# Placing gate passes after each half of a column tile, in a gated recurrence followed by a multiplicative feed-forward

## The chip, the core and the metric

The kernel runs on one core of a Trainium2 chip. The metric is device time in microseconds (us) of one execution. Engines are named as in the profile: PE (TensorE matmul, with PEld for its weight loads), DVE (VectorE), ACT (ScalarE), POOL (GpSimd), SP (SyncE, which here issues nearly all DMAs).

## The reference, cut to what matters

Batch 4, 8 heads, 768 positions, head dimension 48. A recurrence with a complex gate per position and row, then a feed-forward of two products multiplied together:

```python
mag = np.sqrt(a_re * a_re + a_im * a_im)
scale = np.minimum(mag, 0.999) / (mag + 1e-06)
a_re_n, a_im_n = (a_re * scale, a_im * scale)
for t in range(S):
    ar, ai = (a_re_n[:, :, t, :, None], a_im_n[:, :, t, :, None])
    new_re = ar * S_re - ai * S_im
    new_im = ar * S_im + ai * S_re
    kv = np.einsum('bhd,bhe->bhde', k[:, :, t], v[:, :, t])
    S_re, S_im = (new_re + kv, new_im)
    y[:, :, t] = np.einsum('bhd,bhde->bhe', q[:, :, t], S_re)
# x = y as (3072 tokens, 384)
a = x @ w1            # 384 x 1024
b = x @ w2
out = (a * b @ w3) @ w_out
```

The weights come as 64-bit floats; the rest is float32.

## The kernel before

The recurrence is solved in closed form over a **unit** of 384 positions (half a sequence of one batch; 8 units, `NU`; "tile u" or "unit u" below). The running product of gate magnitudes is a scan, the running sum of gate angles is another, and with k divided and q multiplied by the running product and both turned by the angle, the recurrence becomes a masked product of q and k. The feed-forward's w3 and w_out are multiplied into one matrix `w3o` beforehand, in the prologue.

**What PE does for a unit** (`pieces`, L1108): per chunk of 128 positions (3, `UC`) two transposes `tp` of the turned keys (`turn`, L724), copied by ACT into `KT` (L733); the state product `kv` (`state`, L787; its sum `T` is made by DVE at L802, or by an ACT copy at L800); scores `sc` (`scores`, L736; DVE puts them under the mask at L748); outputs `y` (`outputs`, L760; ACT copies them into `xT`, L781). `tp`, `kv` and `y` share two PSUM buffers, so each needs the reader of the one before the last to be done. Odd units have no state product for the last chunk.

**The feed-forward of the unit before** is laid between these pieces: `ffn_ab` (L813), 8 column tiles, each two groups of three 128x384 matmuls (L820; w1 first, then w2), an ACT copy `a` (L825) and a DVE product `ab` (L826), in four PSUM buffers; then the output product. For unit 0 that is three chunks of 8 matmuls (`ffn_out`, L901, L909); for later units the last chunk so, and the first two by seven smaller products `p` (`out_pair`, L851, L873), for which DVE first makes four sums `So` (L848) and adds the results (L855).

**Gates** of the next unit (`gates`, L563) run on ACT and DVE meanwhile, whole passes over 128x1152 elements (unit 0: three parts of 384). Each is yielded with its engine, an estimated cost, a name and the names that it waits for. Their order before: Ln and Exp of re (names a1, r1; `act`, L576), im/re (L591), range looks on re (`low`, ACT, `check_gates`, L548, into Z), square and maximum (L598), Ln (z1), n (L608), z2, a2, z3 on ACT, min (L619), three scans (mag, L624), Ln and Exp of the running product (l, e: the `gR` rows of L576), q (L636), z4 (L638), r2 (L640), k (L642), three tiny copies (ends, L645), table load and arctangent (at, L648), three angle scans (ang, L655), turns (ACT) and z5 (L667), abs, cos, sin (ACT), then kc, qc, ks, qs (L682 to L691). The load of the next `re` follows the angle scans, of the next `im` kc and qc. Then 12 DMAs move the results into `KL` and `QL` (`move`, L701), and k and q of the next unit are loaded.

**What sets the order.** PE's order is written out by hand. In the prologue the other engines are ordered by the framework's scheduler from the order of emission. From the end of unit 0's pieces on, all engines follow the order in which `run` (L1171) emits: it walks the list of PE items; after each it emits gate passes as long as a planner with clocks per engine (costs in `TIMES`, L1142, and in the yields) finds that the pass starts before the next item's PE work ends and is done before its engine is next asked for (`fits`, L1226). So gate passes stand only between items, and `ab`, with both its groups, is one item. `AHEAD` says how many items of the feed-forward come before the unit's first piece; `HEAD` how many `ab` items come before unit 1. Each engine runs its queue in that order.

**Prologue** (to 85.5 us): eight rows of w3 and w_out are converted from 64-bit words (ACT L955, L958; DVE L951, L953, L961, L963, L965) and multiplied by PE (`fuse`, L1070) while unit 0's gates run; then unit 0's pieces with the first gate passes of unit 1 (`step`), and four blocks of w1 and w2 (`w12_work`; `raw` loads at L936), of which the last two are converted within unit 0's feed-forward (kind `abw`).

**Checks.** POOL reads the weights and gates again (`check_weights`) for values outside a range; `judge` (L1078) gathers all tests on DVE, sums them by one small matmul (`count`, L1097) and leaves a verdict in `good`; every engine reads it at the end (L1356), and a general path runs if it is 0.

Of the kernel before, what the change touches and what calls it, by code (L numbers as in the profile page):

```python
# [375 lines left out]
def kernel(  # L376
# [47 lines left out]
    HEAD = 8  # L424
# [6 lines left out]
    AHEAD = [0, 0] + [4] * (NU - 2)  # L431
    LO, HI = 32, D - 32
    PASS, WIDE, SCAN, LAND, SLACK, LATE, RING, LOOK = 1.17, 1.36, 0.97, 1.8, 0.7, 1.2, 8, 4.0
# [114 lines left out]
    def check_gates(u, re, junk, f=0):  # L548
        return [nc.scalar.activation(out=junk, in_=re, func=AF.Relu, scale=scale, bias=bias,
                                     accum_out=st_low[:, x, u, f:f + 1])  # L550
                for x, (scale, bias) in enumerate(((-1.0, LEAST), (1.0, MOST)))]
# [11 lines left out]
    def gates(u, split):  # L563
# [25 lines left out]
        for i, s in enumerate(parts):  # L589
            yield "DVE", WIDE, "im", ("r1", ("im", u))  # L590
            tt(out=im[:, s], in0=im[:, s], in1=r[:, s], op=OP.mult)  # L591
            if u > 1:
                yield "ACT", 2.5, "low", ("r1",)
                check_gates(u, re, Z)
        yield None
        for i, s in enumerate(parts):
            yield "DVE", WIDE, "sq", ("im", "low")
            nc.vector.tensor_tensor_reduce(out=Z[:, s], in0=im[:, s], in1=im[:, s], scale=1.0, scalar=0.0,  # L598
                                           op0=OP.mult, op1=OP.max, accum_out=st_tan[:, u, i:i + 1])
# [17 lines left out]
        for s in parts:  # L617
            yield "DVE", 0.76, "min", ("a2",)
            least = ts(out=A[:, s], in0=A[:, s], scalar1=0.999, scalar2=None, op0=OP.min)  # L619
            if u == 1:  # L620
                tc.add_manual_dep(least.ins, masked[-1].ins.name, ORDER, reason="scores first")
            for f in range(s.start, s.stop):
                yield "DVE", SCAN, "mag", ("min", "z3")
                nc.vector.tensor_tensor_scan(out=A[:, f], data0=A[:, f], data1=Z[:, f], initial=1.0,  # L624
                                             op0=OP.mult, op1=OP.mult)
        yield None
# [7 lines left out]
        for s in parts:  # L634
            yield "DVE", WIDE, "q", ("mag", ("q", u))
            tt(out=q[:, s], in0=q[:, s], in1=A[:, s], op=OP.mult)  # L636
            yield "DVE", WIDE, "z4", ("e",)
            tt(out=Z[:, s], in0=A[:, s], in1=r[:, s], op=OP.mult)  # L638
            yield "DVE", WIDE, "r2", ("z4",)
            stt(out=r[:, s], in0=Z[:, s], scalar=2.0, in1=r[:, s], op0=OP.subtract, op1=OP.mult, reverse0=True)  # L640
            yield "DVE", WIDE, "k", ("r2", ("q", u))
            tt(out=k[:, s], in0=k[:, s], in1=r[:, s], op=OP.mult)  # L642
        yield "ACT", 0.6, "ends", ("k",)
        for X in (R[:, :, TT], K2[:, :, TT], st_dec[:, u]):
            nc.scalar.copy(out=X, in_=A[:, :, TT - 1])  # L645
        yield None
        yield "ACT", 2.45, "at", ("im",)
        chain(nc.scalar.preload_act_table_set("trig_and_small"))  # L648
        for s in parts:
            act(out=im[:, s], in_=im[:, s], func=AF.Arctan)  # L650
        yield None
# [10 lines left out]
        for s in parts:  # L662
            n = re[:, s].bitcast(I32)
            yield "ACT", PASS, "turns", ("ang",)
            act(out=n, in_=Z[:, s], func=AF.Copy, scale=0.5 / PI)
            yield "DVE", WIDE, "z5", ("turns",)
            stt(out=Z[:, s], in0=n, scalar=-2 * PI, in1=Z[:, s], op0=OP.mult, op1=OP.add)  # L667
# [116 lines left out]
    for T in Tb:  # L784
        nc.gpsimd.memset(T, 0.0)
# [27 lines left out]
    def ffn_ab(u, j):  # L813
        if j == 0:
            ab_t[u] = one.tile([P, KF, TT], FP, tag="ab", name="ab")
        got = []
        for w in (w1s, w2s):
            m = ps_m.tile([P, TT], FP, tag="mm", name="m")
            for f in range(KD):
                nc.tensor.matmul(out=m, lhsT=w[:, j * P // WB, f, j * P % WB:j * P % WB + P], rhs=xT_t[u][:, f],  # L820
                                 start=(f == 0), stop=(f == KD - 1))
            got.append(m)
        a = two.tile([P, TT], FP, tag="a", name="a")
        with tc.high_priority():
            nc.scalar.copy(out=a, in_=got[0])  # L825
            nc.vector.tensor_tensor(out=ab_t[u][:, j], in0=got[1], in1=a, op=OP.mult)  # L826
# [278 lines left out]
    for V in Vb:  # L1105
        nc.gpsimd.memset(V, 0.0)

    def pieces(u):  # L1108
# [6 lines left out]
        if u % 2:  # L1115
            return [[("need", u), tr[0][0]], [tr[0][1]], [tr[1][0], kv[0]], [tr[1][1]], [kv[1]], sc[0], sc[1] + [y[0]],
                    sc[2] + [y[1]], [y[2], ("end", u)]]
        return [[("need", u), tr[0][0]], [tr[0][1]], [tr[1][0], kv[0]], [tr[1][1]], [tr[2][0], kv[1]], [tr[2][1]],
                [kv[2]] + sc[0], sc[1] + [y[0]], sc[2] + [y[1]], [y[2], ("end", u)]]

    def ffn(u, parts=1):
        ab = [("ab", lambda j=j: ffn_ab(u, j)) for j in range(KF)]
        last = [("o" if n == parts - 1 else "part", f) for n, f in enumerate(ffn_out(u, UC - 1, parts))]
        if u == 0:
            return ab + [(("part", "o")[n], f) for t in range(UC) for n, f in enumerate(ffn_out(u, t, parts))]
# [5 lines left out]
    def unit(u, rest, ahead):  # L1131
# [5 lines left out]
        first = [i * (len(rest) - 2) // (n - 1) for i in range(n)] + [len(rest)] if u > 1 else [0, 1, 2, 3, 3, 4, 4, 5, 5, 5, 6]  # L1137
# [5 lines left out]
        "ab": (("PE", 1.94), ("ACT", 0.48), ("PE", 1.94), ("DVE", 0.56)),  # L1143
        "abw": (("PE", 1.94), ("ACT", 0.48), ("PE", 1.94), ("DVE", 0.56), ("DVE", 0.56), ("ACT", 1.08), ("DVE", 1.5)),
# [3 lines left out]
        "part": (("PE", 2.58),), "p1": (("PE", 1.3), ("ACT", 0.32)), "p2": (("PE", 1.3),), "p4": (("PE", 1.3),),  # L1148
# [22 lines left out]
    def run(seq):  # L1171

        def item(kind):
# [11 lines left out]
            if k in ("ab", "abw", "so", "spart", "part", "p1", "p2", "p7", "p5"):  # L1185
                wait = held["m"][-4]
                held["m"].append(clock["PE"] + (8.0 if k[0] == "p" else 0.0))
            clock["PE"] = max(clock["PE"], wait)
            for e, d in TIMES[kind]:
                if e != "PE":  # L1190
                    done = max(done, clock["PE"])
                elif k in ("ab", "abw") and done:
                    clock["PE"] = max(clock["PE"], held["m"][-4])
                    held["m"].append(0.0)
# [6 lines left out]
                if e != "PE" and k in ("ab", "abw", "so", "o"):  # L1201
                    held["m"][-1] = done
# [75 lines left out]
    with tc.manual_schedule(engines={mybir.EngineType.PE}):  # L1278
# [36 lines left out]
        for i, p in enumerate(pieces(0)):  # L1315
# [3 lines left out]
            if i in (1, 3, 6, 9):  # L1319
# [6 lines left out]
            step(steps, 5 if i == 0 else i >= 6)  # L1326
            if i in (5, 7):
                work[2 + (i == 7)]()
        with tc.manual_schedule(engines={mybir.EngineType.Activation, mybir.EngineType.DVE, mybir.EngineType.Pool, mybir.EngineType.SP}):
# [4 lines left out]
            def head(i):  # L1334
                rest[i][1]()
                if i in (2, 3):
                    work[2 + i]()
                if i == 4:
# [5 lines left out]
            seq = [("abw" if i in (2, 3) else "ab", lambda i=i: head(i)) for i in range(HEAD)]  # L1344
# [4 lines left out]
            clock.update(POOL=0.0, SP=0.0, DMA=0.0)  # L1349
            ready.clear()  # L1350
            ready.update(at=6.5, r2=6.3, k=7.7)
            advance()
            run(seq[:-6] + [("judge", 0)] + seq[-6:-2] + [("judge", 1)] + seq[-2:])
# [41 lines left out]
```

## Time and profile before

| what | us |
|---|---|
| median of 3 runs (561.05 to 562.63) | 562.1 |
| the profiled execution, its own time | 560.6 |
| its span on the core | 558.7 |
| PE busy | 524.4 |
| last PE matmul ends | 549.96 |

In a row of the profile stand the line of the kernel, the engine, the operation, out<-in with sizes, then busy time and what ended the idle time before it. "issue" is time in which the engine waited for nothing that the profile shows. The slices row gives the busy share in tenths of 40 equal parts of the span. Where PE is idle for a short time its releaser is named, with how long and how often.

### The profile page before, as it was taken

Reading aid. Unit: us, or ns where it says so; the run is one execution under the profiler, and the core shown is the slowest. Engines: PE = TensorE matmul, PEld = TensorE weight load, DVE = VectorE, ACT = ScalarE, POOL = GpSimd, SP = SyncE. Lnnn points to the kernel's source line nnn. Section 1 sums busy time; section 2 is a strip of 40 time slices with the busy share of each in tenths; the row PEclk is TensorE's granted clock in tenths of the full one; section 3 lists DMA queues with packets and bytes.
Section 4 is the critical chain, followed back from the end, with each engine's and each line's share of the span. In section 5 each row is a group of like instructions: output and inputs, shape, how many; then the busy total and the mean of one; then the engine's idle time right before and its main releaser. Section 6 shows DMA issues by size and latency. Waiting matters only on the chain.

```text
span 558.7 us, 13227 instructions
## 1 busy us (share of the span) xinstructions
PE 524.4 (94%) x5474; PEld 358.8 (64%) x5474; DVE 364.0 (65%) x514; ACT 274.8 (49%) x389; POOL 362.7 (65%) x425
## 2 busy tenths in 40 slices
PE   4779889998999999999999999999999999999993
PEld 2345565566656785669666875687567856696572
DVE  7998399778685866687576756695848664421141
ACT  6988766585377325742475237722774242111100
POOL 3000000198888888888899889898998888886000
PEclk9899979999999999999999999999999999999998
DMA  8996978279559626892579245943595228322001
GB/s 260 354 406 166 285 210 279 65 167 196 137 125 242 182 106 174 204 265 77 145 192 222 83 118 152 241 130 102 136 234 156 64 69 212 77 70 70 0 2 49
DMA packets 73190, 89.73 MB, mean 161 GB/s; under 512 B 31776, under 2 KB 62944, under 8 KB 72352
## 3 DMA queue, kind: packets, MB, share of 16 engines
q1 hardware_dynamic: 67040, 69.78, 47.2%
q0 software_dynamic: 6080, 19.01, 11.6%
q8 instruction: 45, 0.74, 0.6%
q14 instruction: 25, 0.20, 0.1%
HBM read 65.14 MB, written 4.72 MB: 125 GB/s over the span
## 4 chain that ended last, share of the span: by engine, by line
PE 79%; DVE 8%; ACT 5%; issue 2%; DMA 2%; SPq 1%; DVEq 0%; ACTq 0%
PE m L820 45%; PE p L873 11%; PE y L779 7%; PE o L909 6%; PE sc L745 5%; DVE So L848 2%; PE kv L796 2%; DVE gA L624 2%; PE tp L731 2%; PE f L1070 1%; ACT gZ L576 1%; ACT low L955 1%; DMA im<-in_a_im_dram 1%; DMA k<-in_k_dram 1%; ACT gR L576 1%
## 5 line engine op out<-in xcount | busy, mean ns | idle before, releaser
L820 PE MATMUL m<-xT,w1s 128*128 128x384 f32 x384 | 135.0, 488 | 0.0
L820 PE MATMUL m<-xT,w2s 128*128 128x384 f32 x384 | 134.3, 486 | 0.0
L820 PEld LDWEIGHTS m<-xT,w2s 128*128 128x128 f32 x384 | 73.0, 190 | 50.9
L820 PEld LDWEIGHTS m<-xT,w1s 128*128 128x128 f32 x384 | 71.4, 190 | 44.9
L826 DVE TENSOR_TENSOR ab<-m,a 128x384 f32<-128x384 f32 x64 | 35.4, 553 | 91.4 <-PE m L820 83.1
L1016 POOL TENSOR_SCALAR look<-look 128x256 f32<-128x256 f32 (+1 forms) x84 | 88.4, 1053 | 7.3
L997 POOL TENSOR_TENSOR seen<-seen,look 128x256 bf16<-128x256 bf16 (+1 forms) x84 | 69.5, 828 | 6.8
L825 ACT COPY a<-m 128x384 f32<-128x384 f32 x64 | 30.3, 473 | 77.8 <-PE m L820 77.8
L981 POOL MEMSET seen<- 128x256 bf16 x1 | 0.3, 312 | 101.9 <-DVE w2s L965 101.9
L1013 POOL TENSOR_TENSOR look<-look 128x256 f32<-128x256 f32 (+1 forms) x72 | 59.5, 826 | 1.9
L909 PE MATMUL o<-w3o,ab 128*128 128x384 f32 x160 | 54.1, 487 | 0.0
L1015 POOL TENSOR_SCALAR look<-look 128x256 f32<-128x256 f32 (+1 forms) x44 | 50.4, 1146 | 5.1 <-DMA look<-in_a_re_dram 1.9
L781 ACT COPY xT<-y 128x384 f32<-128x384 f32 x24 | 11.4, 477 | 76.6 <-PE y L779 76.6
L992 POOL DMA_DIRECT2D look<-in_w_dram x56 | 33.6, 599 | 16.6 <-POOL seen L997 16.6
L733 ACT COPY KT<-tp 128x384 f32<-128x384 f32 x40 | 34.0, 856 | 18.1 <-PE tp L731 17.9
L1018 POOL TENSOR_TENSOR look<-look 128x256 f32<-128x256 f32 (+1 forms) x44 | 39.4, 896 | 3.7
L748 DVE COPY_PREDICATED A<-mask,sc 128x512 f32<-128x512 uint8 x48 | 33.0, 732 | 13.3 <-PE sc L745 12.8
L909 PEld LDWEIGHTS o<-w3o,ab 128*128 128x128 f32 x160 | 29.5, 190 | 18.3 <-issue 0.2
L779 PE MATMUL y<-A,V 128*32 128x128 f32 x768 | 40.2, 278 | 0.0
L1070 PE MATMUL f<-wo_s,w3s 128*128 128x384 f32 x96 | 37.2, 534 | 1.6 <-issue 1.6
L745 PE MATMUL sc<-QL,KL 96*32 96x32 f32 (+3 forms) x1536 | 33.5, 239 | 4.1 <-DVE A L748 1.9
L745 PEld LDWEIGHTS sc<-QL,KL 96*32 96x32 f32 x1536 | 29.2, 112 | 10.6 <-DVE A L748 4.4
(121 smaller groups left out, 904.7 us busy)
## 6 DMA issues: line engine op xcount, KB each, us to landing
look<-in_w_dram POOLq DMA_DIRECT2D x56, 256.0 KB, 3.5
raw<-in_w_dram SPq DMA_DIRECT2D x6, 1024.0 KB, 10.2
raw<-in_w_dram SPq DMA_DIRECT2D x8, 768.0 KB, 8.9
KL<-gR SPq DMA_DIRECT2D x24, 192.5 KB, 5.0
KL<-k SPq DMA_DIRECT2D x24, 192.5 KB, 5.6
re<-in_a_re_dram SPq DMA_DIRECT2D x24, 192.0 KB, 3.4
im<-in_a_im_dram SPq DMA_DIRECT2D x24, 192.0 KB, 3.3
k<-in_k_dram SPq DMA_DIRECT2D x24, 192.0 KB, 8.8
```

Source lines behind the costliest of these rows:

```text
L745: nc.tensor.matmul(out=sc[SB * g:SB * g + SB, j, s0:C], lhsT=KL[:, x * n + j, w][:, s0:s0 + SB], rhs=QL[:, x * n + j, w][:, s0:C], start=T ...
L779: nc.tensor.matmul(out=o, lhsT=a, rhs=b, start=s0, stop=s1)
L820: nc.tensor.matmul(out=m, lhsT=w[:, j * P // WB, f, j * P % WB:j * P % WB + P], rhs=xT_t[u][:, f], start=(f == 0), stop=(f == KD - 1))
L826: nc.vector.tensor_tensor(out=ab_t[u][:, j], in0=got[1], in1=a, op=OP.mult)
L873: nc.tensor.matmul(out=m[p], lhsT=a[:, f], rhs=b[:, f], start=(f == 0), stop=(f == KH - 1))
L909: nc.tensor.matmul(out=m, lhsT=ab_t[u][:, f, t * P:(t + 1) * P], rhs=w3o[:, f], start=(f == 0), stop=(f == KF - 1))
L997: nc.gpsimd.tensor_tensor(out=seen[:, 0:n], in0=seen[:, 0:n], in1=x, op=OP.add)
L1013: tt(out=x, in0=x, in1=x, op=OP.mult)
L1015: ts(out=y, in0=x, scalar1=high, scalar2=None, op0=OP.is_le)
L1016: ts(out=x, in0=x, scalar1=low, scalar2=None, op0=OP.is_ge)
L1018: tt(out=x, in0=x, in1=y, op=OP.mult)
L1070: nc.tensor.matmul(out=sums[j], lhsT=w3_t[f][:, j * P:(j + 1) * P], rhs=w3_t["wo"][:, f], start=(f == 0), stop=(f == KF - 1))
```

## The change

Each group of three matmuls of `ffn_ab` becomes an item of its own ("ab1" with the ACT copy, "ab2" with the product), so that the planner may put gate passes and pieces after either. `HEAD` and `AHEAD` now count halves; some costs and start clocks of the planner are changed. In the gates: the two range looks go from behind r1 to the scans, one after each of the first two, and write their junk into the `gR` buffer; for units from 1 on, the table load and arctangent stand right behind l and e, followed by z4 and r2; k, q and the three tiny copies come after the angle scans and the turns pass. In unit 0, q comes after k. In `pieces` the last two outputs of a unit stand together. Output chunks in two parts get the kind "half". The verdict's tests are emitted before the `ab2` group of column tile 6, and its count before that of column tile 7, in the last unit's feed-forward. Two memsets on POOL clear only the columns that no load writes.

```diff
-    HEAD = 8
+    HEAD = 16
-    AHEAD = [0, 0] + [4] * (NU - 2)
+    AHEAD = [0, 0, 12, 10] + [8] * (NU - 4)
-    PASS, WIDE, SCAN, LAND, SLACK, LATE, RING, LOOK = 1.17, 1.36, 0.97, 1.8, 0.7, 1.2, 8, 4.0
+    PASS, WIDE, SCAN, LAND, SLACK, LATE, RING, LOOK = 1.17, 1.4, 1.05, 1.8, 0.7, 1.2, 8, 4.0
...
-            if u > 1:
-                yield "ACT", 2.5, "low", ("r1",)
-                check_gates(u, re, Z)
...
-            yield "DVE", WIDE, "sq", ("im", "low")
+            yield "DVE", WIDE, "sq", ("im",)
...
+                if u > 1 and f < 2:
+                    yield "ACT", 1.25, "low", ("im",)
+                    check_gates(u, re, r, f)
...
-        for s in parts:
-            yield "DVE", WIDE, "q", ("mag", ("q", u))
-            tt(out=q[:, s], in0=q[:, s], in1=A[:, s], op=OP.mult)
+        def spread(s):
             yield "DVE", WIDE, "z4", ("e",)
             tt(out=Z[:, s], in0=A[:, s], in1=r[:, s], op=OP.mult)
             yield "DVE", WIDE, "r2", ("z4",)
             stt(out=r[:, s], in0=Z[:, s], scalar=2.0, in1=r[:, s], op0=OP.subtract, op1=OP.mult, reverse0=True)
+
+        def scaled(s):
             yield "DVE", WIDE, "k", ("r2", ("q", u))
             tt(out=k[:, s], in0=k[:, s], in1=r[:, s], op=OP.mult)
+            yield "DVE", WIDE, "q", ("mag", ("q", u))
+            tt(out=q[:, s], in0=q[:, s], in1=A[:, s], op=OP.mult)
...
+        early = u > 0
+        if early:
+            yield "ACT", 2.45, "at", ("im",)
+            chain(nc.scalar.preload_act_table_set("trig_and_small"))
+            bent(parts[0])
+            yield from spread(parts[0])
+            yield None
+        else:
+            for s in parts:
+                yield from spread(s)
+                yield from scaled(s)
+            yield from ends()
...
             yield "ACT", PASS, "turns", ("ang",)
             act(out=n, in_=Z[:, s], func=AF.Copy, scale=0.5 / PI)
+            if early:
+                yield from scaled(s)
+                yield from ends()
...
-        nc.gpsimd.memset(T, 0.0)
+        nc.gpsimd.memset(T[:, :, D:64], 0.0)
...
+        return [("ab1", lambda: half(w1s)), ("ab2", lambda: half(w2s))]
...
-                    sc[2] + [y[1]], [y[2], ("end", u)]]
+                    sc[2] + [y[1], y[2], ("end", u)]]
...
-        "ab": (("PE", 1.94), ("ACT", 0.48), ("PE", 1.94), ("DVE", 0.56)),
+        "ab1": (("PE", 1.94), ("ACT", 0.48)), "ab2": (("PE", 1.94), ("DVE", 0.56)),
...
-            if i in (1, 3, 6, 9):
+            if i in (1, 3, 6, 8):
...
-            step(steps, 5 if i == 0 else i >= 6)
+            step(steps, 5 if i == 0 else (i >= 6) + (i == 8))
...
-            clock.update(POOL=0.0, SP=0.0, DMA=0.0)
+            clock.update(DVE=5.0, POOL=0.0, SP=0.0, DMA=0.0)
             ready.clear()
-            ready.update(at=6.5, r2=6.3, k=7.7)
+            ready.update(ang=8.0)
             advance()
-            run(seq[:-6] + [("judge", 0)] + seq[-6:-2] + [("judge", 1)] + seq[-2:])
+            run(seq[:-12] + [("judge", 0)] + seq[-12:-10] + [("judge", 1)] + seq[-10:])
```

## The prediction, made before the changed kernel was run

> **What bounds the kernel now.** I read the busy table first, then stages of PE's busy time, then PE's waits, then the chain of waits inside the stages with idle time.
>
> ```profile
> PE 524.4 (94%) x5474; PEld 358.8 (64%) x5474; DVE 364.0 (65%) x514; ACT 274.8 (49%) x389; POOL 362.7 (65%) x425
> ...
> PE   4779889998999999999999999999999999999993
> ```
>
> PE is the bound: 34.3 us of the 558.7 us span are not PE. The change leaves every matmul in place, so it can win only idle PE time. Where is that? Busy time by stage (columns: stage, then its length and PE busy):
>
> ```profile
> 0.00:85.50 85.50, 65.97 (x643) 40.36 (x644) 70.61 (x141) 65.95 (x102) 5.24 (x12) 0.92 0.91 276
> 85.50:116.50 31.00, 31.00 (x98) 18.28 (x97) 26.17 (x35) 18.46 (x26) 6.67 (x8) 1.00 0.46 152
> 116.50:148.00 31.50, 28.56 (x542) 20.26 (x541) 24.94 (x26) 16.92 (x21) 27.79 (x32) 1.00 0.88 201
> 148.00:208.20 60.20, 59.24 (x684) 41.91 (x683) 40.74 (x49) 33.61 (x48) 53.24 (x60) 1.00 0.61 156
> 208.20:266.80 58.60, 58.60 (x662) 41.40 (x661) 40.90 (x48) 29.27 (x40) 51.25 (x59) 1.00 0.67 178
> 266.80:327.30 60.50, 59.26 (x683) 41.93 (x683) 40.82 (x49) 31.11 (x43) 54.04 (x60) 1.00 0.60 153
> ```
>
> Idle: 19.5 us in the prologue; 2.9 in column tile 1 (116.5 to 148); 1.0 in tile 2; none in tile 3; 1.2 in tile 4. Tiles 5, 6, 7 by the same view: 0, 0.8, 0. The end, from the last matmul (549.96) to 558.7, is 8.7. PE's waits (total, times, longest):
>
> ```profile
> PE sc L1070 <- DVE wo_s L965: 14.1, 4, 7.6
> PE kv L796 <- ACT KT L733: 4.1, 4, 1.2
> ```
>
> The first is the prologue (weight rows not yet converted). The second is the even tiles plus 1.2 at 66. The chain of waits at tile 4 (start, length, what):
>
> ```profile
> 301.17 2.89 DVE So L848 x3
> 304.06 0.90 DVE gA L619
> ...
> 307.16 1.37 DVE gA L624
> 308.53 0.02 issue
> 308.55 1.17 ACT gR L576
> 309.72 0.20 ACT U L878
> 309.92 0.76 ACT KT L733
> 310.68 0.04 issue
> 310.72 0.88 PE kv L796 x48
> ```
>
> VectorE's four `So` passes put the gate scans late; ScalarE's log (gR, L576) waits for the last scan; the small KT copy stands behind the log, and PE's kv behind KT. Tile 1 is different: its first scores wait for a DMA, the last move of KL and QL.
>
> **What the Trainium skill says.** "Perfetto Trace Analysis", section Tensor Engine Instruction: ACT, DVE and GPSIMD are strict FIFO. The trace agrees: KT's transpose ended before 308.55 and its copy ran at 309.8 behind the log. "Runtime: NRT & Kernel Launch", section Instruction fetch mechanics: instructions arrive in 16 KiB blocks of 256 by a DMA queue, the next while the current one runs. Agreed here: queue q8 has 45 packets, 0.74 MB, 16.4 KB each; and PE pauses in tile 1 with "issue" as the only cause at 135.8, 139.3 and 143.3, resuming at 136.2, 140.2 and 144.2: 4.0 us apart, 128 matmuls and 128 weight loads between. The same section gives PE room for 2048 instructions; these pauses don't fit that. "DMA: Bandwidth & Descriptors", section Queues, rings and completion order: on each DMA engine a queue's descriptors are consumed in ring order. So what SP issues first delays what it issues next.
>
> **The change part by part.** Times are of the profiled execution, 560.6 us (span 558.7 and 1.9 around it); the median shown is 1.5 above it, and I add the difference found to the median.
>
> *Even tiles, 2, 4, 6.* With halves as units the last transposes stand between `ab` halves or `p` products, and the gate passes run earlier against PE: in the new order `low` (2 x 1.25) no longer precedes `sq`, the scans of tiles 4 and 6 stand ahead of `So`. Tile 4: PE is at transpose 11 about 29 us into its unit (14 halves of 1.94, 3 transposes of 0.36, kv 0.85), KT11 is copied by 30.8, kv1 starts at 31.7. The log comes after two `low` passes and the copy of transpose 20, at 34.7; log and exp 1.17 each, table load 1.28, arctangent 1.17: ScalarE is free at 39.5. The o group ends at 39.6, its copy takes 0.48, KT21 ends at 41.0, and kv2 comes after a p product at 41.5. Margin 0.5 us. Tile 2: the log is placed after all KT copies; KT21 ends at 42.4 against kv2 at 42.7. Tile 6 is like 4, with the scans 0.5 later. Each stall goes: minus 1.0, 1.2, 0.8 = minus 3.0. Next late there would be that same KT copy. Both ends: minus 3.2 (nothing left) and minus 1.5 (half returns).
>
> *Tile 1's gates.* This is the costly part.
>
> ```profile
> 87.49 1.36 DVE L636 TENSOR_TENSOR q<-q,gA 128x1152 f32<-128x1152 f32 x1
> 90.12 1.36 DVE L638 TENSOR_TENSOR gZ<-gA,gR 128x1152 f32<-128x1152 f32 x1 [1.27 <-ACT gR L576]
> ...
> 108.07 1.36 DVE L667 SCALAR_TENSOR_TENSOR gZ<-re,gZ 128x1152 f32<-128x1152 int32 x1
> ```
>
> Before, q runs at 87.49 while ScalarE makes the exponential VectorE waits for: free. After, q stands among the ab products behind k, in a stretch where VectorE (90 to 108) only pauses 1.44 us for weight conversion copies. Adding start-to-start gaps of the rows in the new order: z4, r2, ab 3.13; three scans and copy 2.87; conversions, products, k and q up to the z5 pass: 13.3 with the same 1.44 of pauses. z5 starts at 109.4, 1.3 later. z5, abs, cos, kc, qc follow serially (6.65 from 108.07 to qc's end at 114.72), so qc ends 1.3 later. On SP's queue stand im x3, KL x6, QL x6, issued without a gap from 114.78 to 124.65; all come 1.3 later, and the first scores (131.00, 0.8 after PE was ready) too.
>
> Then ScalarE: `z1` now stands ahead of KT01. It waits for im's landing, im and sq (to 124.0), so KT01 ends at 126.5 (123.9 before), kv0 at 127.4, KT10 behind z2 at 128.8, transpose 11, four o matmuls (2.6), kv1 (0.85): scores at 132.7. Plus 1.7 in all. Below: 0.4 if fetch pauses shrink as much; above: 2.5.
>
> *SP's order.* The next `re` load (3 issues, 0.61 each) moves ahead of the fourth weight block and waits for the scans (96.1). The block, issued at 87.1 before, goes out at 98.1; the smallest landing time in the raw row is 5.3, so 103.4, wanted at 103.2: plus 0.1, in the 1.7. With the row's median, 8.9, it lands at 107.0: that is a rival.
>
> *Prologue.* Tile 0 has k before q. A scan (0.95) moves behind the fifth row's conversion: PE starts that row about 0.8 earlier than 39.7. But the table load (1.28, at 52.88 before) and a sine now precede the copy of the last output-weight row: that row's VectorE pass ends at 55.2 against 54.6, so plus 0.6 at the transposes. ScalarE then does a1 and r1 together ahead of two KT copies, which gives 0.5 back to the chain (r1, im, sq, z1, n, T, mask) that frees the scores at 73.2. Net plus 0.1, between minus 0.7 and plus 0.8. The POOL memsets shrink (T 1.44, V 2.69 at 1.7 to 5.8): their first readers come after 31, so nothing.
>
> *y1 and y2 together.* y2 needs the last mask: scores' end plus two copies of 0.73, behind y1's 1.76. Hidden unless a gate pass (1.36) stands between; the order has none. PE's stream gets denser: 192 matmuls in 4.9 us. Taken as plus 0.0, up to the second rival.
>
> *Verdict in the last ffn.* Its 14 small VectorE passes (538.6 to 540.5) and the 0.12 us count matmul move ahead of the `p` group. The answer was ready at 547.5 against the last product's 549.96 before: never last. Nothing; 0.3 either way.
>
> Sum: -3.0 + 1.7 + 0.1 = -1.2 us: 559.4 against 560.6, or 560.9 against the median.
>
> **Rivals.** *The delay of tile 1 is absorbed* (chance 0.33): the pauses for instructions in tile 1 (0.4, 0.9, 0.9) shrink as PE arrives later and finds blocks loaded. -1.2 - 1.7 = -2.9: 559.2. For it: the pauses are 2.2 us. Against: the V loads that crowd the DMA engines (busy share 0.88) shift with it.
>
> *Instruction blocks arrive late in every tile* (0.12; slower). `re` loads (3 x 192 KB) now fall into the scores and y stage, where PE takes 384 instructions in 4.9 us. At tile 1's pause of 0.9 in six tiles, +5.4 - 1.2 = +4.2: 566.3. It turns the sign past 1.2 us and shows as slower past 2.9, some three tiles. Against: in tile 3 scores and y already ran 256 instructions in 3.0 us without a pause.
>
> *The fourth weight block is late* (0.07; slower): 3.8 us at the z5 pass, passed on to tile 1's scores: +2.6, 564.7.
>
> *The copies still queue* (0.06): the 0.5 and 0.3 us margins of KT21 fail; +1.8, 563.9.
>
> **How the numbers follow.** 0.3% (1.7 us) is about what a measurement of this kernel can tell from no change. The forecast, 560.9 (0.42), has its own range 559.6 to 562.3, inside that bound but for a tail of 0.05 below. Faster: 0.33 + 0.05 = 0.38; same 0.37; slower 0.12 + 0.07 + 0.06 = 0.25. The range 558.2 to 565.0 takes in all but most of the second rival and a few hundredths below.
>
> **What would show it.** Right: no wait of kv on KT in tiles 2, 4, 6 (about 59.3 us a tile instead of 60.3); z5 of tile 1 later by 1.3 and its first scores by 1.7; fifth row earlier, last row later. Wrong: scores of tile 1 on time; "issue" pauses between y1 and y2; a wait for `raw` near 103; kv waiting for KT at all.

## The result and the profile after

The changed kernel takes 560.4 us (median of 12 runs, 557.85 to 563.03) against 562.1 us of the kernel before (12 runs beside it): ratio 0.9965, 95% interval 0.9946 to 0.9985. Its profiled execution takes 559.57 us, its span is 557.6 us. The forecast was 560.9. The time is right; most of the way to it is not, as the profile shows. Lines of the changed kernel are some 20 to 25 higher than before: kv is L818, the KT copy L755, the scores L767, the exit L1413, the read of the verdict L1378.

From the page, busy time and PE's slices:

```profile
PE 522.5 (94%) x5474; PEld 359.5 (64%) x5474; DVE 358.7 (64%) x514; ACT 273.0 (49%) x389; POOL 359.8 (65%) x425
...
PE   5789869997899999999999999999999999999995
```

PE's busy time by stage, for the stretches that answer to those shown of before (from one unit's feed-forward to the next; columns: stretch, its length and PE busy, then the other engines, granted clock, DMA share, GB/s):

```profile
0.00:85.86 85.86, 64.43 (x643) 40.05 (x644) 70.17 (x142) 66.48 (x102) 2.36 (x12) 0.94 0.90 275
85.86:117.75 31.89, 31.22 (x97) 18.16 (x96) 24.43 (x33) 18.34 (x26) 5.61 (x8) 1.00 0.45 147
117.75:151.87 34.12, 28.77 (x541) 20.34 (x540) 21.20 (x23) 15.89 (x21) 29.64 (x40) 1.00 0.84 192
151.87:212.26 60.39, 59.24 (x684) 42.17 (x683) 39.77 (x48) 32.33 (x44) 52.05 (x62) 1.00 0.65 164
212.26:270.44 58.18, 58.18 (x661) 41.41 (x661) 45.23 (x52) 31.72 (x42) 51.68 (x54) 1.00 0.65 172
270.44:330.14 59.70, 59.25 (x685) 42.12 (x683) 44.42 (x54) 32.06 (x46) 53.68 (x56) 1.00 0.64 163
...
388.90:447.81 58.91, 58.90 (x684) 42.02 (x683) 38.88 (x48) 28.58 (x41) 52.81 (x57) 1.00 0.58 145
```

Tile 1 (rows two and three) takes 66.0 us, against 62.5 before; tile 2 takes 60.4 (60.2); tile 4 59.7 (60.5), tile 6 58.9 (60.1). The last matmul ends at 551.7, against 549.96 before. **PE finishes 1.8 us later than before, and yet the span is 1.0 us shorter (558.68 and 557.65).** PE's waits in the changed kernel (total, times, longest):

```profile
PE sc L1095 <- DVE wo_s L990: 14.2, 5, 6.5
PE sc L767 <- DVE A L770: 5.0, 4, 2.2
PE tp L753 <- ACT KT L755: 2.8, 2, 1.4
PE kv L818 <- ACT KT L755: 1.9, 2, 1.0
PE y L801 <- issue: 1.8, 3, 1.1
PE sc L767 <- DMA QL<-q: 0.7, 1, 0.7
```

None of the two waits of kv on KT stands in tiles 2, 4 or 6: one is in the prologue, one in tile 1. That part of the change works. But in their place tile 2 has 0.7 for the last move of QL and 0.4 for instructions, tile 4 has 0.4 for instructions, and tile 1 has grown.

Where does the gain come from? From what follows the last matmul: 8.7 us before, 5.9 now. The exit of the kernel before, then its read of the verdict (count, shortest/median/longest in ns, first and last start in us):

```profile
L1391 POOLq EVENT_SEMAPHORE  x4: 17/17/17, 557.9 to 558.6; - x4
L1391 POOLq DRAIN  x3: 40/107/6933, 550.9 to 558.4; - x3
L1391 SPq DRAIN  x3: 7/7/13, 555.3 to 558.1; - x3
```

```profile
L1356 POOLq TENSOR_LOAD <-good x1: 502/502/502, 547.5 to 547.5; - x1
...
L1356 DVEq TENSOR_LOAD <-good x1: 541/541/541, 550.0 to 550.0; - x1
```

GpSimd reads the verdict at 547.5, branches at 548.1, and runs the first instruction after the branch at 550.8; then comes a DRAIN of 6.93 us, from 550.9 to 557.8. Its next semaphore is at 557.9, and the barrier ends at 558.7: from reading the verdict to the end 11.2 us. VectorE, which reads it at 550.0, after its last sum, and SyncE, whose drains begin at 555.3, are long done. The same rows of the changed kernel, in the same two views:

```profile
L1413 POOLq EVENT_SEMAPHORE  x4: 17/17/17, 556.9 to 557.5; - x4
L1413 POOLq DRAIN  x3: 40/107/6933, 538.9 to 557.4; - x3
L1413 SPq DRAIN  x3: 7/7/13, 556.8 to 557.1; - x3
...
L1413 DVEq DRAIN  x2: 10/14/17, 555.4 to 557.1; - x2
```

```profile
L1378 POOLq TENSOR_LOAD <-good x1: 502/502/502, 535.7 to 535.7; - x1
...
L1378 DVEq TENSOR_LOAD <-good x1: 544/544/544, 551.8 to 551.8; - x1
```

The same 6.93 us now run from 538.9 to 545.8, beside PE's work. What ends last now is SyncE. VectorE's last sum starts at 551.75; SyncE issues the last output transfer behind it, branches at 552.5, runs its first instruction after the branch at 555.4, then a row of waits for semaphores, and reaches its drain at 556.8. GpSimd's semaphore answers at 556.9, and the end is at 557.6, 5.1 us after SyncE's branch. VectorE, which reads the verdict at 551.8, stands at its drain at 555.4, 1.4 us before SyncE.

### The profile page after: what moved, and what is told of

It reads as the page before. It is cut to its first block, busy times and chain, and to the rows that moved or that the text cites. A ratio compares the mean times of both kernels' runs of the same rounds, so it can differ in the third digit from the quotient of the medians.

```text
span 557.6 us, 13220 instructions
## 1 busy us (share of the span) xinstructions
PE 522.5 (94%) x5474; PEld 359.5 (64%) x5474; DVE 358.7 (64%) x514; ACT 273.0 (49%) x389; POOL 359.8 (65%) x425
## 3 DMA queue, kind: packets, MB, share of 16 engines
q1 hardware_dynamic: 67040, 69.78, 47.7%
## 4 chain that ended last, share of the span: by engine, by line
PE 72%; DMA 8%; DVE 7%; ACT 6%; issue 3%; SPq 2%; ACTq 0%; DVEq 0%
PE m L843 37%; PE p L898 11%; PE o L934 7%; PE y L801 6%; PE sc L767 5%; DMA KL<-k 3%; DMA QL<-q 2%; PE tp L753 2%; ACT low L980 2%; PE kv L818 2%; ACT gZ L575 1%; PE f L1095 1%; SPq L506 1%; DMA raw<-in_w_dram 1%; DMA k<-in_k_dram 1%
## 5 line engine op out<-in xcount | busy, mean ns | idle before, releaser
L843 PE MATMUL m<-xT,w1s 128*128 128x384 f32 x384 | 134.7, 487 | 0.7 <-ACT a L848 0.7
L843 PEld LDWEIGHTS m<-xT,w2s 128*128 128x128 f32 x384 | 71.4, 190 | 46.2
L1041 POOL TENSOR_SCALAR look<-look 128x256 f32<-128x256 f32 (+1 forms) x84 | 91.5, 1089 | 7.3
L1022 POOL TENSOR_TENSOR seen<-seen,look 128x256 bf16<-128x256 bf16 (+1 forms) x84 | 78.2, 931 | 6.8
L1038 POOL TENSOR_TENSOR look<-look 128x256 f32<-128x256 f32 (+1 forms) x72 | 53.5, 743 | 2.6 <-DMA look<-in_w_dram 0.8
L1040 POOL TENSOR_SCALAR look<-look 128x256 f32<-128x256 f32 (+1 forms) x44 | 45.8, 1041 | 5.3 <-DMA look<-in_a_re_dram 2.1
L1043 POOL TENSOR_TENSOR look<-look 128x256 f32<-128x256 f32 (+1 forms) x44 | 38.3, 871 | 3.7
L767 PE MATMUL sc<-QL,KL 96*32 96x32 f32 (+3 forms) x1536 | 32.7, 235 | 6.7 <-DVE A L770 5.0
L801 PE MATMUL y<-QL,T 96*32 96x128 f32 x640 | 36.7, 280 | 0.2 <-issue 0.2
L755 ACT COPY KT<-tp 128x384 f32<-128x384 f32 x40 | 34.0, 856 | 5.4 <-PE tp L753 5.4
L767 PEld LDWEIGHTS sc<-QL,KL 96*32 96x32 f32 x1536 | 28.5, 110 | 12.7 <-DVE A L770 6.5
## 6 DMA issues: line engine op xcount, KB each, us to landing
re<-in_a_re_dram SPq DMA_DIRECT2D x24, 192.0 KB, 3.3
im<-in_a_im_dram SPq DMA_DIRECT2D x24, 192.0 KB, 3.6
k<-in_k_dram SPq DMA_DIRECT2D x24, 192.0 KB, 8.8
```

The source lines that it names most:

```text
L755: nc.scalar.copy(out=KT_t[u, c][:, :, :, x].rearrange("p h d f -> p f d h"), in_=tp.rearrange("p f (d h) -> p f d h", h=H))
L767: nc.tensor.matmul(out=sc[SB * g:SB * g + SB, j, s0:C], lhsT=KL[:, x * n + j, w][:, s0:s0 + SB], rhs=QL[:, x * n + j, w][:, s0:C], start=T ...
L801: nc.tensor.matmul(out=o, lhsT=a, rhs=b, start=s0, stop=s1)
L1022: nc.gpsimd.tensor_tensor(out=seen[:, 0:n], in0=seen[:, 0:n], in1=x, op=OP.add)
L1038: tt(out=x, in0=x, in1=x, op=OP.mult)
L1040: ts(out=y, in0=x, scalar1=high, scalar2=None, op0=OP.is_le)
```

## Experiments

Every ratio is to the kernel before, run beside it. A tile is measured from the start of one unit's feed-forward to the next, in one profiled execution of each run; that execution lay up to 3.1 us below the run's median (run 11: 558.6 against 561.7), so a few tenths in one tile prove little unless other runs repeat them. "First scores" of tile 1 are counted from the start of unit 0's feed-forward: 45.6 us before, 48.5 in the changed kernel.

**1. The verdict late in the changed kernel.**

```diff
-            run(seq[:-12] + [("judge", 0)] + seq[-12:-10] + [("judge", 1)] + seq[-10:])
+            run(seq[:-6] + [("judge", 0)] + seq[-6:-2] + [("judge", 1)] + seq[-2:])
```

> The changed kernel with the verdict alone put back: its tests before the last o group's products, its count matmul after the o group, as in the kernel before. Theory (the verdict was on the path): what ends last is not the last product but GpSimd, which after reading the verdict takes the branch (0.5 + 2.7 us) and then drains for 6.93 us, and 0.8 us later the span ends; 11.2 us from reading the verdict to the end. The last matmul stays at 551.7, the verdict is read by GpSimd at about 549.3 and the span grows from 557.6 to 560.5, so the median from 560.4 to about 563.3. Rival (the prediction's step, worth nothing): the end hangs on the last product, span and median stay within 0.3 us.

563.55 us; ratio 1.0015 (0.9997 to 1.0034). Exit and read of the verdict in this kernel:

```profile
L1413 POOLq DRAIN  x3: 40/107/6933, 554.0 to 561.5; - x3
```

```profile
L1378 POOLq TENSOR_LOAD <-good x1: 498/498/498, 550.5 to 550.5; - x1
```

From reading to the end (span 561.8) it is 11.3 us again. The tail after the last matmul is 8.9 us, 3.0 more than in the changed kernel, and the median is 3.2 above that kernel's. The last matmul came at 552.9, 1.2 later than expected, and the read with it. The rest of the change, without the verdict, shows no gain.

**2. The verdict early in the kernel before.** Column tiles are whole there, so the tests stand ahead of tile 6 and the count ahead of tile 7.

```diff
-            run(seq[:-6] + [("judge", 0)] + seq[-6:-2] + [("judge", 1)] + seq[-2:])
+            run(seq[:-11] + [("judge", 0)] + seq[-11:-10] + [("judge", 1)] + seq[-10:])
```

> The kernel before with the verdict alone moved forward: its tests before column tile 6 and its count before column tile 7 of the last feed-forward; nothing else is changed. Theory (the verdict was on the path): the last matmul stays at 550.0 (0.2 either way), GpSimd's drain begins at about 537 and is long over; then VectorE is last, which reads the verdict after its last sum at 550.0 and ends 5.8 us later as in the changed kernel: span 555.8, 2.9 less; median about 559.2, at or below the whole change. Rival: median stays at 562.1, within 0.3.

558.91 us; ratio 0.9936 (0.9912 to 0.9959). The last matmul is at 550.7 and the span 557.1; GpSimd's drain starts at 536.6. The tail is 6.4 us instead of 8.7. It is 0.6 longer than expected: SyncE, last here too, runs its first instruction 3.4 us after its branch (551.5 to 554.9), not 2.9 as in the changed kernel. One line brings as much as the whole change or more; the two directions together settle the verdict.

**3. Unit 1's gates in the old order, the rest of the change kept.**

```diff
-        early = u > 0
-        if early:
+        if u == 1: yield "DVE", WIDE, "q", ("mag", ("q", u)); tt(out=q, in0=q, in1=A, op=OP.mult)
+        if u > 1:
...
-            yield "DVE", WIDE, "q", ("mag", ("q", u))
-            tt(out=q[:, s], in0=q[:, s], in1=A[:, s], op=OP.mult)
+            if u != 1: yield "DVE", WIDE, "q", ("mag", ("q", u))
+            if u != 1: tt(out=q[:, s], in0=q[:, s], in1=A[:, s], op=OP.mult)
...
-            ready.update(ang=8.0)
+            ready.update(at=6.5, r2=6.3, k=7.7)
```

> The changed kernel with the gates of unit 1 alone in the order of the kernel before (q ahead of z4, then k and the ends, arctangent after them, the angle scans after unit 0's feed-forward begins, so that the fourth weight block is fetched ahead of the next re). Theory (the moves of unit 1 cost what the halves bring): the pass z5 of tile 1 comes at 108.1 instead of 110.1, the first scores at about 131.5 instead of 134.3, and tile 2's wait for QL (0.7) and tile 1's wait for the product copy (0.7) go with it; last matmul 2.5 to 3.5 us earlier than 551.7, median about 557.4. Rival (the delay comes from z1 standing ahead of the KT copies and from the halves themselves): first scores no earlier than 133.3 and the median 559.4 or more.

558.56 us; ratio 0.9932 (0.9908 to 0.9956). First scores after 45.4 us, tile 1 62.2 us, last matmul 547.4. The late first scores come from unit 1's new order. The median came out 1.2 above the expected one, because the expected gain in tile 2 didn't come: the wait for QL is gone, but tile 2 still takes 60.3. PE's only wait there:

```profile
PE sc L767 <- issue: 1.2, 1, 1.2
```

**4. The fourth weight block ahead of the next re, all passes in place.**

```diff
-        if 1 < u + 1 < NU:
+        if 1 < u < NU - 1:
             load_gates(u + 1, ("re",), ("ang",))
...
-            work[4](False)
+            work[4](False); load_gates(2, ("re",))
```

> The changed kernel with two entries of SP's queue exchanged: the fetch of the fourth weight block goes out before the load of unit 2's re, with all passes in place. Theory A (the block is late because re waits for the scans in front of it): VectorE's 1.25 us wait at its first pass on the block goes, z5 comes at 108.9 instead of 110.1, first scores 1.2 earlier at about 133.1; median about 559.2. Theory B (late passes of VectorE hide behind the copies and the fetch pauses of PE): scores within 0.3 of 134.3, median 560.4.

560.86 us; ratio 0.9967 (0.9948 to 0.9986), the time of the changed kernel. Neither theory in full: VectorE's wait for the block is gone (z4 to z5 19.3 us, not 20.7), and first scores come after 47.7 us instead of 48.5; but PE then pauses longer in the scores and outputs (1.8, 0.9 and 0.6 against 0.5, 0.9 and 1.1), and tile 1 takes 66.1. What is left of z4 to z5, 1.4 us over the 17.95 of before, is the q pass (1.36).

**5. Column tiles whole again.** The two halves as one item, its costs as before, HEAD 8, AHEAD 6, 5 and then 4; the rest of the change stays. The main line of the edit:

```diff
-        return [("ab1", lambda: half(w1s)), ("ab2", lambda: half(w2s))]
+        return [("ab", lambda: (half(w1s), half(w2s)))]
```

> The changed kernel with the headline part undone: each column tile of the feed-forward is one item again (both products together, HEAD 8 and AHEAD in whole tiles), while the order of the gate passes, the place of the range looks, y1 with y2, and the early verdict stay. Theory (the halves free the KT copies): waits of kv on KT come back in tiles 2, 4 and 6, some 0.8 to 1.2 us each; tile 6 goes from 58.9 back to about 60; the median from 560.4 to about 562. Rival (the halves bring nothing; tiles are within 0.3 of the changed kernel's): 560.4.

582.12 us; ratio 1.0353 (1.0306 to 1.0401), far outside both theories. The longest wait of PE in the tiles:

```profile
PE tp L753 <- DVE gR L704: 11.8, 5, 2.6
```

The keys themselves (kc, L704) come too late in five units, and in tile 3 the scores wait 3.6 us more, until the last move of QL lands. That the planner with whole tiles finds too few places for the new order of passes is the likely reason; no run shows it apart. With this planner the halves are needed for that order; what they bring to the old one this run cannot say.

**6. The old gate order for all units from 1 on, halves kept.** The edit of run 3 with `u > 0` and never the early branch.

> The changed kernel with the gate passes of all units from 1 on in the order of the kernel before (q first, z4, r2, k, ends, then the arctangent), halves, range looks, y1 with y2 and early verdict kept. With unit 1 alone put back the median was 558.6 and tile 2 still took 60.3 us: the wait of kv for KT is gone there and PE stands 1.2 us at the first scores with nothing shown but an instruction block on its way, while the DMA engines are busy to 90% and over because the moves and the k, q loads of the unit end some 4 us later than before. Theory A (late transfers crowd the instruction block): with k and q early again the moves of tile 2 start 3 to 4 us earlier after its start, the engines are quiet at its first scores, the pause goes and tile 2 takes 59.2; with tile 4 the median falls to about 557. Theory B (the pause belongs to where the block's edge falls in PE's stream, which is the same): tile 2 stays at 60.3 and the median at 558.6. Theory C (the new gate order is what frees the KT copies): waits of kv on KT return, even tiles 60 and more, median 559.5 or more.

564.34 us; ratio 1.0048 (1.0028 to 1.0068). It doesn't test theory A: the planner put the arctangent late, and the moves of tile 2 start 25.8 us after its feed-forward (23.6 in the changed kernel), not earlier. Tile 2 pauses 1.4 for instructions and takes 60.5; tile 3 takes 64.3 instead of 58.2, where transposes wait 2.4 for kc and the outputs pause 1.7 for instructions. Theory C's price is met, but not its mechanism: no wait of kv on KT stands in tiles 2, 4, 6. So the new order is not what removes those waits; the halves with the moved range looks do it with the old order too.

**7. Without GpSimd's reading of the weights,** on run 3's kernel; all but the gates' looks are left out.

```diff
-        for w in (w1, w2, w3t, wo):
+        for w in ():
```

> As the kernel with unit 1's gates put back, but it leaves out GpSimd's reading of the weights for the range test (72 loads of up to 256 KB on its own DMA queue from 153 us on; the gates are still looked at). It is no candidate but a measure of contention. Theory A (crowded DMA engines delay PE's instruction blocks): that queue holds some 25% of the engines around the first scores of tile 2; without it the pauses there (1.2) and in tile 4 (0.9 and 0.6) fall to half or less, so tile 2 takes at most 59.7, median 557.5 or less. Theory B (pauses come from elsewhere): tile 2 stays at 60.3, median 558.6.

554.48 us; ratio 0.9873 (0.9843 to 0.9904). Tile 2 takes 58.9 and tile 4 59.1, with no pause. But VectorE's busy time also fell, from 359.9 to 336.7, so this alone doesn't say whether transfers or slow passes were the cause.

**8. The control: the same left out of the kernel before with the early verdict.**

> The kernel before with the verdict moved forward, and it leaves out GpSimd's reading of the weights for the range test, as the run with unit 1's gates put back did; it is the control of that run. There the even tiles fell by 1.5, 1.2 and 0.1. Theory A (the late gate passes of the change bring transfers to the scores, which then delay PE's instruction blocks): in the order of before the transfers end earlier and no pause stands in tiles 2, 4, 6, only the wait of kv for KT, about 1.0 each; that wait stays, tiles 2, 4, 6 stay at 60.2, 60.4, 60.1 within 0.3, and only tile 1 and the prologue may gain; median 557.5 or more against 558.9. Theory B (the reading costs every order alike): even tiles fall by about 1 us each, median 555.5 or less.

557.05 us; ratio 0.9923 (0.9895 to 0.9950). The median lies between the theories; on the tiles A fell: 59.4, 59.2 and 59.2 for tiles 2, 4, 6, and the waits of kv on KT are gone there too. The reason stands in VectorE's groups (150 to 500 us), first of the kernel before, then of this run (busy us, mean ns):

```profile
L624 DVE TENSOR_TENSOR_SCAN gA<-gA,gZ 128x384 f32<-128x384 f32 x15 | 17.9, 1245 | 0.5
...
L848 DVE TENSOR_TENSOR So<-ab 128x512 f32<-128x512 f32 x12 | 10.0, 832 | 0.2
```

```profile
L624 DVE TENSOR_TENSOR_SCAN gA<-gA,gZ 128x384 f32<-128x384 f32 x15 | 13.3, 940 | 0.5
...
L848 DVE TENSOR_TENSOR So<-ab 128x512 f32<-128x512 f32 x12 | 8.2, 688 | 0.2
```

Beside GpSimd's reading these scans and sums run a third and a fifth longer; the late scans in front of the log, from which the waits on KT came, were partly GpSimd's doing.

**9. GpSimd's passes kept, their loads left out,** on run 3's kernel.

```diff
-            got = late.tile([P, 512], FP, tag="look", name="look", bufs=LOOKS)
+            got = late.tile([P, 512], FP, tag="look", name="look", bufs=LOOKS) if group[0] == "gate" else had[-LOOKS]
+            had.append(got)
...
-                nc.gpsimd.dma_start(out=got.bitcast(I32)[:, 0:group[2]], in_=group[1])
+                pass
```

> As the kernel with unit 1's gates put back; GpSimd's passes over the weights stay as they are, but run on buffers loaded earlier: the 72 DMA loads for them are left out, and the verdict doesn't depend on their count. Leaving out passes and loads together gave 554.5 against 558.6, but took two things away at once: 11% of the DMA time, and GpSimd's passes, beside which VectorE's passes ran longer (scans 1102 ns against 943, q and k passes 1600 and 1544 against 1350, 23 us in all). Theory A (the DMA engines are the shared thing): the pause at tile 2's first scores (1.2) goes as it did there, tile 2 takes 59.2 or less, median 556.5 or less, while VectorE stays at about 360 us busy. Theory B (VectorE's slower passes put the transfers late): VectorE's 360 us and the pause stay, tile 2 at 60 or more, median about 558.6.

557.10 us; ratio 0.9917 (0.9885 to 0.9949). This separates the two: VectorE stays at 358.2 us busy, the scans at 1084 ns, and still tile 2 takes 58.9 us with no pause. The DMA engines' busy share from 186 to 196 us in 40 slices (tenths), first in run 3 (first scores at 191.1), where PE stood from 192.2 to 193.4, then here (first scores at 192.2):

```profile
DMA  9999999999899999999999886976599999995210
```

```profile
DMA  9999999846991000000000000000395259999840
```

With quiet DMA engines PE crosses its instruction blocks in these scores without a stop. The packets of the two traces show the block itself: on the instruction queue q8 a packet of 16 KB starts 43.4 us after tile 2's feed-forward in run 3, lands at 192.0, and PE goes on at 193.4; here it starts 40.0 us after it, and nothing stops. The median came out 0.6 above the expected bound. In this profile tile 1 took 64.9 us, with 1.6 for a KT copy and 1.5 at its first masks; there too an instruction packet had landed 1.4 us before PE went on. (GpSimd's loads of the weights start after tile 1.)

**10. y1 and y2 apart again,** on run 3's kernel.

```diff
-                    sc[2] + [y[1], y[2], ("end", u)]]
+                    sc[2] + [y[1]], [y[2], ("end", u)]]
...
-            step(steps, 5 if i == 0 else (i >= 6) + (i == 8))
+            step(steps, 5 if i == 0 else i >= 6)
```

> As the kernel with unit 1's gates put back, with the last two outputs of a unit apart again, one product of the feed-forward between them as before. Theory A (the prediction's step: standing together they cost and bring nothing): median 558.6, tiles within 0.3. Theory B (together they save odd tiles 0.3 us each, 58.5 to 58.2): odd tiles at 58.5 again, median about 559.5. Theory C (together they crowd PE's instruction blocks): tiles 2 and 4 about 1 us shorter, median 557.

559.59 us; ratio 0.9979 (0.9956 to 1.0002). Odd tiles take 58.8, 59.1 and 58.5 instead of 58.2, 58.3 and 58.2, but tile 4 only 59.2 instead of 60.3. Theory B for the odd tiles, something of C for one even tile; the intervals of the two ratios just touch (0.9956).

**11. More feed-forward ahead of the pieces,** on run 3's kernel.

```diff
-    AHEAD = [0, 0, 12, 10] + [8] * (NU - 4)
+    AHEAD = [0, 0, 14, 12] + [11] * (NU - 4)
```

> As the kernel with unit 1's gates put back, with more of the feed-forward laid ahead of each unit's pieces (14, 12 and then 11 halves for 12, 10 and 8), so that the first scores come later against the transfers. Theory A (what counts is whether the moves and loads are done when PE runs through instruction blocks in the scores): pauses in tiles 2 and 4 fall below 0.5, tiles 2 and 4 take 59.3 or less, median about 557. Theory B (gate passes of the next unit wait for the pieces, so everything shifts together or comes too late): tiles 2 and 4 at 60 or more, odd tiles wait for late keys, median 559.5 or more.

561.70 us; ratio 0.9995 (0.9972 to 1.0018). The pause in tile 2 fell to 0.7, tile 2 to 60.0 and tile 4 to 58.9, but tile 3 rose to 62.3, with one pause of 2.0 for instructions at its outputs; PE's granted clock is then 0.65 for the next 4 us, which is most of what the pause doesn't explain. Neither theory holds in every tile; the median is B's.

**12. Only q and the block put back in unit 1.** The early arctangent stays.

```diff
-        early = u > 0
-        if early:
+        if u == 1: yield "DVE", WIDE, "q", ("mag", ("q", u)); tt(out=q, in0=q, in1=A, op=OP.mult)
+        if early := u > 0:
...
+            if u != 1: yield "DVE", WIDE, "q", ("mag", ("q", u))
...
-            work[4](False)
+            work[4](False); load_gates(2, ("re",))
```

> The changed kernel with two things of unit 1 alone put back: q is multiplied in VectorE's gap ahead of z4, and the fourth weight block is fetched before the next re. The early arctangent and the rest of unit 1's order stay; the planner then lays z5 two conversions earlier by itself. Theory A (q and the block are what tile 1 lost): first scores at most 45.6 us after unit 0's feed-forward begins (48.5 in the changed kernel, 47.7 with the block alone, 45.4 with unit 1's old order), tile 1 about 62.5 us, median about 558.6. Theory B (z1 ahead of the KT copies and the halves cost the most): first scores no earlier than 47, tile 1 at least 64.5, median 560 or more.

553.81 us; ratio 0.9869 (0.9838 to 0.9899): the best of all complete kernels, well below the changed kernel and run 4, and below run 3 (0.9908 to 0.9956). First scores come after 46.1 us, between the two theories, and tile 1 takes 62.7, as theory A has it; the median is far below A's. VectorE's timeline of this kernel (start, busy, what):

```profile
87.17 1.36 DVE L653 TENSOR_TENSOR q<-q,gA 128x1152 f32<-128x1152 f32 x1
89.80 1.36 DVE L635 TENSOR_TENSOR gZ<-gA,gR 128x1152 f32<-128x1152 f32 x1 [1.27 <-ACT gR L575]
...
100.37 1.35 DVE L689 SCALAR_TENSOR_TENSOR gZ<-re,gZ 128x1152 f32<-128x1152 int32 x1
...
110.35 1.35 DVE L706 TENSOR_TENSOR gA<-q,re 128x1152 f32<-128x1152 f32 x1
```

q runs in the gap before z4, as before the change, and z5 takes the place that q had among the products: 10.6 us after z4, not 20.7. qc is done at 111.7 instead of 116.9, and the last of unit 1's moves is issued by 121.4 instead of 127.0. In tile 2 the moves begin 21.1 us after its feed-forward, not 23.6, the DMA engines are nearly quiet when its first scores begin (191.0), and PE waits for nothing: 58.9 us. Of the 5.3 us between this span and the changed kernel's, 1.2 lie in the prologue, which varies by itself (below); tile 1 and tile 2 bring 4.8.

## Why the prediction was right and wrong

The sum was -1.2 us; the two profiled executions differ by -1.0, their spans as much. The span's difference is made up so: prologue +0.5, tile 1 +3.5, even tiles -1.8, odd tiles -0.4, the end -2.8. Four of the prediction's terms were off, and it was luck that they cancelled.

- **Even tiles, -3.0.** The waits went as said: no kv waits on KT in tiles 2, 4, 6. The size was -1.8: +0.2, -0.8 and -1.2. What was named as next late (the KT copy of the third chunk) was not: transfers and instruction blocks were. Runs 6 and 8 add that the waits also go without the new order, and without GpSimd's reading in the kernel before. In tile 2 the chain of the changed kernel runs through the last move (start, length, what):

```profile
185.81 10.34 DMA QL<-q
196.14 0.14 issue
196.28 1.56 PE sc L767 x56
```

- **Tile 1's gates, +1.7.** Measured +2.9 at the first scores and +3.5 over the tile. Of z4 to z5 (17.95 to 20.67 us, +2.7) the q pass was rightly priced, 1.36. The term that failed is SP's order, "plus 0.1" (the prediction's own figures, 103.4 against 103.2, give 0.2): the smallest landing time of the raw row was taken, 5.3; it was 6.57, and VectorE stood 1.25 us (below). The earlier z4 gives back 1.1. From z5 to the scores it is +1.3, priced at 0.4: the last move of QL lands 7.9 us after its issue (126.3 to 134.2), where it took 6.8 before (124.0 to 130.9), and the scores start 0.1 us behind it in both. The pauses in the scores and outputs take 0.6 more than before. The chain of the changed kernel, then the row of the three last moves (median us from issue to landing), before and after:

```profile
97.37 6.57 DMA raw<-in_w_dram
103.94 0.02 issue
103.96 0.57 DVE low L976
```

```profile
QL<-q SPq DMA_DIRECT2D x3, 192.0 KB, 6.6
```

```profile
QL<-q SPq DMA_DIRECT2D x3, 192.0 KB, 7.6
```

  The profile names a load of k as what these scores wait for; that load lands at 134.7, after they have begun.
- **Prologue, +0.1.** +0.5 in the profile (85.38 to 85.86). The fifth row began 1.3 earlier (39.7 to 38.4; 0.8 foreseen), and the last row not later (0.6 foreseen). Nothing can be read from the sum: among the runs with the changed prologue unit 0's feed-forward began between 83.5 and 86.7.
- **y1 and y2 together, nothing.** Run 10: it is worth some 0.3 to 0.8 in each odd tile, and may have cost tile 4 about 1. In the changed kernel tiles 3 and 7 are 0.3 shorter (58.5 to 58.2), as in the other runs that keep the two together.
- **Verdict, "Nothing; 0.3 either way".** This is the step that failed worst: -2.8. The argument compared the answer at 547.5 with the last product at 549.96 and stopped there. It left out what GpSimd has to do after it reads the answer: a branch of 2.7 us and a drain of 6.93. Run 1 shows what the forecast was worth without the verdict: it gave -1.2 for the rest, and the rest is between nothing and +0.3%.
- **Rivals.** Late instruction blocks were given for every tile, at 0.9; outside tile 1 they came in tiles 2, 4 and 5 of the changed kernel, by 0.4, 0.4 and 0.2 us. The weight block came late by a third of what its rival said. The pauses in tile 1 didn't shrink: 1.9 us before (0.4, 0.9, 0.6), 2.5 after (0.5, 0.9, 1.1; the profile names a mask for the middle one, but it too ends 1.5 us after an instruction packet has landed).

The chance for faster was 0.38; the measured interval (-0.5% to -0.15%) straddles the bound of 0.3%. That the number fits says nothing for the reasons.

Open: what the halves, and what the moved range looks, bring each by itself, and why tile 4 pauses in some orders and not in others. Run 12 without its reordered load was not tried; nor was a kernel with k and q loaded after the scores, nor one whose weight checks are loaded by another engine than GpSimd.

## What to carry to other kernels

The end of a kernel is a stage of its own: look at every engine's last read, branch and drain, not at the last product; a scalar that each engine reads before it leaves must be ready earlier than the slowest exit is long. When a pass moves, ask what it takes the gap from and which load stands behind it in its queue; one pass of 1.36 us put back into a real gap, with one load reordered (worth nothing alone, run 4), took the ratio from 0.9965 to 0.9869, nearly three times what the whole change had brought. A stall removed from one engine shows up at the next shared thing, here the DMA engines, where PE's own instructions travel too.

## What the runs showed of the hardware

- GpSimd's longest DRAIN at the exit takes 6933 ns in all eleven kernels that keep its loads of the weights, whether it starts at 538.9 or at 554.0; those of the other engines take 7 to 17 ns. In runs 7, 8 and 9, where GpSimd issues 12 loads instead of 84, it takes 1057 ns; the row is run 9's, which keeps the passes:

```profile
L1416 POOLq DRAIN  x3: 40/107/1057, 533.5 to 552.4; - x3
```

  So it goes with the loads that GpSimd has issued in the whole kernel, not with its passes. By these two figures a load costs some 82 ns (an estimate: 5876 ns over 72 loads); whether loads, packets or bytes count isn't shown. The Trainium skill, "VectorE: DVE Perf Modes", section "The DRAIN you can't avoid", gives about 12 ns for such DRAINs on all engines; for GpSimd the measurement decides.
- After the branch at the exit, the first instruction of GpSimd comes 2.5 us after the branch's start (536.3 to 538.8 in the changed kernel), SyncE's and VectorE's 2.9 us (552.5 to 555.4, 552.4 to 555.3), though the branch itself is given as 45 to 72 ns. Over all runs it is 2.5 to 2.9 for GpSimd and 2.9 to 3.8 for the other two. The Trainium skill, "Runtime: NRT & Kernel Launch", section "Instruction fetch mechanics", says that a taken branch to a block that isn't loaded waits for its fetch; the trace agrees with that: an 8 KB packet of the instruction queue q14 moves at 537.3, and three between 552.8 and 554.1.
- GpSimd's passes lengthen VectorE's passes over SBUF. With passes and loads left out, the scans go from 1245 to 940 ns, the sums So from 832 to 688, and 24 us of VectorE's busy time are gone; products and masks that read PSUM keep their time (ab 553 against 556 ns). The Trainium skill, "SBUF — State Buffer", section "SBUF: two separate sides", says that the two engines share a pair of ports; the run with the passes but without their loads agrees: scans still 1084 ns.
- PE's instruction blocks come late where the DMA engines are full: 1.2 us at a busy share of nine tenths in tile 2's first scores, none in the same stage where the share was near zero just before. In all fourteen traces, from unit 0's feed-forward on, all 43 pauses of PE with "issue" as their cause end 1.3 to 1.6 us after a 16 KB packet of q8 has landed.
- A pause can cost more than its length: after run 11's 2.0 us in tile 3 the granted clock was 0.65 for 4 us. Length alone doesn't decide: after 2.6 us in run 5's tile 4 it was 1.00.
